# A convolution + GELU feed-forward kernel: block 0's x in half rows, W_in issued behind the mask, its copies split, and the first second-products moved ahead

## The chip, the cores and the metric

The kernel runs on one core of one Trainium2 chip. The metric is the device time in microseconds (us) of one execution of the program. "Span" is the time from the first to the last instruction in a profiled execution; the device time is about 1.7 us longer (682.34 against 680.6 in the first profile). All timed runs that are compared were fast, with a granted TensorE clock of 0.997 to 1.0. Each round of experiments ran on one chip together with its own runs of the kernel before, but the rounds used four different chips, so profiles of different rounds also differ in the chip. On one of these chips alone, 11 runs of the kernel before spread from 682.18 to 683.73 us.

## The reference

Eight sequences of 4096 tokens with 192 features pass a causal convolution of seven taps, one softmaxed set of weights per group of 24 features. The result goes through a feed-forward layer with an exact GELU.

```python
# x: (8, 4096, 192) f32, weight: (8, 7), w_in: (192, 2048), w_out: (2048, 192)
w = softmax(weight, axis=-1)
x_pad = concatenate([zeros((B, 6, D)), x], axis=1)
y[b, s, h, g] = sum_k w[h, k] * x_pad[b, s + k, h, g]      # the convolution
h = y.reshape(32768, 192) @ w_in                            # first product
out = gelu(h) @ w_out                                       # second product
```

## The kernel before

The tokens are two halves of 16384, and a block takes the same stretch of both: the first six blocks have 256 tokens of each half, the others 512. For each block, VectorE transposes x (32x32 blocks), the convolution makes `xc`, TensorE makes `hp` (first products), ScalarE the GELU `gT`, TensorE the second products in `ob`. Blocks 0 and 1 are convolved on TensorE (the "taps", `pconv`), block 2 onwards on VectorE: seven taps, 21 instructions a block.

The parts that the change and the argument touch, with cuts marked:

```python
def load(e, n, qs=(0, 2, 1, 3), sm=None):            # x of block n, four DMAs
    ...
        if n == 0:                                    # whole rows of 8 tokens, 96 columns of them not used
            dst = [[TB // 32 * DQ, 32], [1, mb * D - DQ]]
            src = [[mb * D, 32], [1, mb * D - DQ]]
        else:                                         # half rows of 384 bytes
            dst = [[TB // 32 * DQ, 32], [DQ, mb], [1, DQ]]
            src = [[D, 32], [32 * D, mb], [1, DQ]]

# GpSimd
win_in(FP[0], FP[1], S_WIN[0])                        # first pair of W_in's DMAs (f32 to bf16 on the way)
g.wait_ge(S_MSET, 1)
... affine_select x2 ...                              # the identity mask
for i in range(1, 3): win_in(FP[i], FP[i + 1], S_WIN[i])
halo(0); halo(1); ... casts of block 1 ...; casts of W_out

# VectorE
for p in range(NP): trans(0, p)
conv_out(v, 0, 1); conv_out(v, 0, 4)
dup(0); dup(1)                                        # copies of W_in to the other 64 partitions
for p in range(NP): trans(1, p)
dup(2)                                                # twice as wide
for j in range(len(PIECES)): conv_out(v, 1, j)        # evictions of block 1's taps
... then blocks 2, 3, ...: trans, 21 conv instructions ...

# SP (sync)
load(sp, 0, (0, 1)); sp.wait_ge(S_WIN[0], 32); load(sp, 1)
for i in range(4): ... W_out, a quarter each ...
load(sp, 2); load(sp, 3); ...

# TensorE
for i in range(NSL[n]):                               # 8 groups of a 256-token block
    mm1(n, i)                                         # 12 first-product matmuls
    for q in behind.get((n, i), []): pconv(*q)        # block 1's taps behind groups 4 and 5 of block 0
    for un in todo[a0:a1]: mm2(n - 1, *un)            # second products of the block before, by shares
```

`S_...` are semaphores. A first-product group writes one of two `hp` buffers, so group i waits for the GELU of group i - 2.

## Time and profile before

| | before |
|---|---|
| device time, median of 3 (then of 6) runs | 683.0 us (682.67 us) |
| span of the first profile | 680.6 us |
| chain that ended last | PE 98% |
| block 1's first group starts | 18.34 us |
| block 2's first group starts | 28.87 us |

The page shows what bounds the kernel as a whole: TensorE (PE). The prediction below quotes that page and the start of the chain. Two more views of the same profile matter for what follows, and the prediction did not use them.

The first is the table by stretches of the kernel before. Its columns are the stretch in us, its length, the busy time of PE, PEld, DVE, ACT and POOL (with counts), the granted clock, the mean busy share of the 16 DMA engines, and GB/s. Queues overlap, so the share can pass 1.

```profile
2.00:5.00 3.00, 3.00 (x8) 1.06 (x7) 2.05 (x10) 2.18 (x6) 2.85 (x7) 1.00 0.97 249
5.00:8.00 3.00, 2.71 (x42) 1.52 (x44) 1.58 (x4) 1.17 (x3) 2.19 (x7) 1.00 1.26 157
...
11.00:14.00 3.00, 2.53 (x38) 1.62 (x38) 1.23 (x3) 2.98 (x4) 0.64 (x2) 1.00 1.02 320
...
17.00:20.00 3.00, 2.59 (x50) 2.00 (x48) 2.11 (x7) 2.73 (x4) 1.31 (x3) 1.00 1.31 232
20.00:23.00 3.00, 3.00 (x70) 2.86 (x66) 2.96 (x9) 2.24 (x3) 0.32 (x1) 1.00 0.38 71
```

From 2 to 20 us the DMA engines are busy throughout (0.97 or more in every stretch, the two not shown here included); only then do they fall to 0.38.

The second is the timeline of the kernel before (start in us, length in us, engine, line, operation, count; in brackets the idle time of the engine just before and what ended it), where block 2 is made on VectorE and taken by TensorE:

```profile
19.24 1.35 DVE L529 STREAM_TRANSPOSE xT<-xin 128x256 f32<-128x256 f32 x3 [0.77 <-DMA xin<-in_x_dram]
27.35 1.27 DVE L562 SCALAR_TENSOR_TENSOR xc<-xT,wcol,acc 128x256 bf16<-128x256 f32 x3
28.87 0.82 PE L763 MATMUL hp<-xc,win 64*128 64x256 bf16 x12
```

VectorE waited for x of block 2 until 19.24, was busy without a gap for 9.38 us (until 27.35 + 1.27 = 28.62), and TensorE took the result at 28.87 without having waited. The two engines came to that point within 0.1 us of each other (VectorE by 28.78, as worked out under Theory A below); the chain view names only the one that came last.

### The profile page before, as it was taken

How to read it: one execution, taken by the hardware profiler on the slowest of the kernel's cores; microseconds unless marked ns; L12 is line 12 of the kernel's file. 1: busy time of each engine (PE TensorE's matmuls, PEld its weight loads, DVE VectorE, ACT ScalarE, POOL GpSimd, SP SyncE). 2: the span in 40 equal slices, each digit the busy share in tenths (PEclk: the TensorE clock that was granted, in tenths of full speed). 3: DMA queues.
4: the chain of work that ended last, by engine and by line, in shares of the span. 5: the costliest groups of instructions: out<-in, count | busy, mean ns of one | idle time of the engine just before them, and what ended most of it. 6: DMA issues, size and time to landing. Idle time of an engine off the chain costs nothing.

```text
span 680.6 us, 27316 instructions
## 1 busy us (share of the span) xinstructions
PE 674.6 (99%) x12576; PEld 407.5 (60%) x12576; DVE 561.7 (83%) x906; ACT 536.5 (79%) x548; POOL 38.9 (6%) x57
## 2 busy tenths in 40 slices
PE   8999999999999999999999999999999999999998
PEld 4999655555555555555555555555555555555557
DVE  6999989888889888899888898888898888988611
ACT  6899987787787877787777788777778777778772
POOL 5126000000000000000000000000000000000000
PEclk9999999999999999999999999999999999999999
DMA  9446233134442133331244422334322444310123
GB/s 223 88 99 138 64 71 81 43 69 95 96 94 61 45 87 94 95 89 46 59 95 94 94 70 45 78 94 96 89 56 47 95 94 96 80 40 25 48 50 94
DMA packets 132994, 54.79 MB, mean 81 GB/s; under 512 B 126480, under 2 KB 132752, under 8 KB 132880
## 3 DMA queue, kind: packets, MB, share of 16 engines
q1 hardware_dynamic: 130960, 51.50, 32.6%
q8 instruction: 98, 1.61, 1.0%
q0 software_dynamic: 1248, 0.79, 0.9%
q10 hardware_dynamic: 672, 0.76, 0.4%
q14 instruction: 16, 0.13, 0.1%
HBM read 28.66 MB, written 25.17 MB: 79 GB/s over the span
## 4 chain that ended last, share of the span: by engine, by line
PE 98%; ACT 1%; DMA 1%; DVE 0%; SPq 0%; issue 0%; ACTq 0%
PE hp L763 48%; PE ob L823 43%; PE ob L793 5%; PE hp L793 1%; DMA xin<-in_x_dram 1%; ACT gT L684 1%; PE ob L714 0%; ACT xc L191 0%; DVE xT L529 0%; ACT xTb L633 0%; SPq L871 0%; DVE osb L283 0%; SPq L332 0%; ACTq L632 0%
## 5 line engine op out<-in xcount | busy, mean ns | idle before, releaser
L684 ACT ACTIVATE gT<-hp 128x1024 bf16<-128x1024 f32 x512 | 523.2, 1024 | 129.0 <-PE hp L763 125.7
L763 PE MATMUL hp<-xc,win 64*64 64x512 bf16 (+2 forms) x6048 | 418.6, 366 | 1.5 <-ACT gT L684 1.1
L823 PE MATMUL ob<-gT,wout 64*64 64x512 bf16 x5376 | 366.3, 376 | 0.0
L562 DVE SCALAR_TENSOR_TENSOR acc<-xT,wcol,acc 128x512 f32<-128x512 f32 (+1 forms) x495 | 314.5, 699 | 0.0
L763 PEld LDWEIGHTS hp<-xc,win 64*64 64x64 bf16 (+1 forms) x6048 | 187.6, 106 | 136.1 <-ACT gT L684 2.6
L823 PEld LDWEIGHTS ob<-gT,wout 64*64 64x64 bf16 x5376 | 172.1, 118 | 123.0
L314 DVE STREAM_TRANSPOSE osb<-ob 128x512 f32<-128x512 f32 x84 | 74.1, 885 | 99.9 <-PE ob L823 99.9
L529 DVE STREAM_TRANSPOSE xT<-xin 128x512 f32<-128x512 f32 (+1 forms) x105 | 78.5, 797 | 3.4 <-DMA xin<-in_x_dram 3.4
L562 DVE SCALAR_TENSOR_TENSOR xc<-xT,wcol,acc 128x512 bf16<-128x512 f32 (+1 forms) x99 | 65.1, 712 | 0.0
L450 POOL COPY xT<-xT 128x18 f32<-128x18 f32 x30 | 27.9, 929 | 505.3 <-DVE xT L529 483.0
L793 PE MATMUL ob<-wout,gT 64*128 64x192 bf16 x896 | 46.8, 243 | 0.0
L793 PEld LDWEIGHTS ob<-wout,gT 64*128 64x128 bf16 x896 | 38.6, 94 | 5.2 <-issue 0.4
L555 DVE TENSOR_SCALAR acc<-xT,wcol 128x512 f32<-128x512 f32 (+1 forms) x90 | 37.5, 473 | 1.1
L698 PE MATMUL hp<-warm 128*128 128x512 bf16 x16 | 5.5, 516 | 1.3 <-DVE warm L466 1.3
L285 ACT ACTIVATE osb<-ob 128x192 f32<-128x192 f32 x2 | 0.7, 331 | 7.1 <-PE ob L793 7.1
L793 PE MATMUL hp<-wout,gT 64*128 64x192 bf16 x128 | 5.9, 243 | 0.0
L283 DVE COPY osb<-ob 128x192 f32<-128x192 f32 x2 | 0.7, 358 | 6.1 <-PE ob L793 6.1
L793 PEld LDWEIGHTS hp<-wout,gT 64*128 64x128 bf16 x128 | 5.3, 94 | 0.0
L657 ACT ACTIVATE acc<-xT,wcol 128x256 f32<-128x256 f32 (+1 forms) x9 | 5.2, 575 | 0.0
L270 ACT ACTIVATE osb<-ob 128x384 f32<-128x384 f32 x10 | 4.9, 486 | 0.0
L698 PEld LDWEIGHTS hp<-warm 128*128 128x128 bf16 x16 | 1.9, 126 | 4.3 <-issue 2.5
L387 POOL DMA_DIRECT2D win<-in_moe_w_in_dram x6 | 3.9, 660 | 0.8 <-POOLq L904 0.8
(36 smaller groups left out, 31.4 us busy)
## 6 DMA issues: line engine op xcount, KB each, us to landing
out_dram<-osb SPq DMA_DIRECT2D x122, 192.0 KB, 3.1
xin<-in_x_dram SPq DMA_DIRECT2D x116, 192.0 KB, 4.1
xin<-in_x_dram SPq DMA_DIRECT2D x20, 96.0 KB, 4.3
woutf<-in_moe_w_out_dram SPq DMA_DIRECT2D x4, 384.0 KB, 5.9
win<-in_moe_w_in_dram POOLq DMA_DIRECT2D x4, 96.0 KB, 4.6
win<-in_moe_w_in_dram POOLq DMA_DIRECT2D x2, 192.0 KB, 5.1
out_dram<-osb SPq DMA_DIRECT2D x8, 48.0 KB, 1.7
out_dram<-osb ACTq DMA_DIRECT2D x4, 96.0 KB, 2.0
```

Of the source, the lines that this page charges most:

```text
L270: e.activation(out=dst, in_=src, func=AF.Copy).then_inc(S_EVA)
L314: v.transpose(ap(osb[m % 2], j, [[8 * C, 128], [C // 2, TB // 32], [NP, 32]]), bank(ring(m, j)),).then_inc(S_EV)
L450: g.tensor_copy(dst, src).then_inc(S_HALO)
L529: v.transpose(ap(xT[n % 2], p * XW + HX, [[NP * XW, 128], [1, w]]), ap(xin[n % NX], p, [[TB // 32 * DQ, 128], [D if n == 0 else DQ, w // 3 ...
L555: ins = v.tensor_scalar(a, src, wk, None, ALU.mult)
L562: ins = v.scalar_tensor_tensor(dst, src, wk, a, op0=ALU.mult, op1=ALU.add)
L657: a.activation(out=acc[n % 2][:, p * TB : p * TB + w], in_=ap(xT[n % 2], p * XW + HX, [[NP * XW, 128], [1, w]]), func=AF.Copy, scale=wcol[ ...
L684: a.activation(out=ap(gT[n % 2], i * c * 2 * w, dst), in_=ap(hp[u % 2], 0, src), func=AF.Gelu,).then_inc(S_GELU)
L698: t.matmul(hp[1][:, 0:512], warm[:, 0:128], warm[:, :])
L763: ins = t.matmul(hp[u % 2][fo : fo + fw, o : o + w], ap(win, f1, [[NP * F, 64], [2, fw]]), xc[n % 2][r, p * TB : p * TB + w], start=(p == ...
L793: ins = t.matmul(bb[sub], gT[m % 2][r, c0 : c0 + 128], wout[r, CH[sub][i] * C : (CH[sub][i] + 1) * C], start=(ph == 0 and i == 0), stop=(p ...
L823: ins = t.matmul(bank(ring(m, j), slice(64 * h, 64 * h + 64), w), ap(wout, 64 * hf * NF * C + CH[h][i] * C + j, [[NF * C, 64], [NP, 64]],) ...
```

## The change

The intent is to shorten the start. Block 0's x is fetched without the columns that nobody uses; GpSimd makes the mask first and issues W_in afterwards; the last, double-width copy of W_in is split in two, with one piece in VectorE's wait ahead of block 1; four of the 16 warm-up matmuls go; and four "units" of second products (8 matmuls) run ahead of block 1's first group, with the chunks of W_out's first half first. The diff, cut to its core:

```diff
-                    dst = [[TB // 32 * DQ, 32], [1, mb * D - DQ]]
-                    src = [[mb * D, 32], [1, mb * D - DQ]]
+                dst = [[TB // 32 * DQ, 32], [DQ, mb], [1, DQ]]
+                    src = [[mb * D, 32], [D, mb], [1, DQ]]
...
-            win_in(FP[0], FP[1], S_WIN[0])
             g.wait_ge(S_MSET, 1)
...
-            for i in range(1, 3):
-                win_in(FP[i], FP[i + 1], S_WIN[i])
...          (in halo(0), behind its memset)
+                    for i in range(3):
+                        win_in(FP[i], FP[i + 1], S_WIN[i])
...
-            dup(0)
-            dup(1)
+            for i in range(3):
+                dup(i)
             for p in range(NP):
                 trans(1, p)
-            dup(2)
+            dup(3)
...
-            for i in range(16):
+            for i in range(12):
...
-            share = {1: [4, 12, 8, 8, 8, 8, 8, 8]}
+            share = {1: [4, 12, 9, 9, 10, 5, 5, 6]}
+            AHEAD = 4
...
+                if m == 0:
+                    us.sort(key=lambda q: not (q[1] == 0 and q[2] < 4))
...
+                if n == 0:
+                    results(0, units(0)[:AHEAD])
```

More of the change, by code (lines that the diff above doesn't have):

```diff
@@ L324, in load @@
                 off = ((q // 2) * HALF + OFF[n]) * D + DQ * (q % 2)
+                dst = [[TB // 32 * DQ, 32], [DQ, mb], [1, DQ]]
                 if n == 0:
-                    dst = [[TB // 32 * DQ, 32], [1, mb * D - DQ]]
-                    src = [[mb * D, 32], [1, mb * D - DQ]]
+                    src = [[mb * D, 32], [D, mb], [1, DQ]]
                 else:
-                    dst = [[TB // 32 * DQ, 32], [DQ, mb], [1, DQ]]
                     src = [[D, 32], [32 * D, mb], [1, DQ]]
@@ L501, in dup @@
             def dup(s):
-                v.wait_ge(S_WIN[s], 32)
+                v.wait_ge(S_WIN[min(s, 2)], 32)
                 for hf in range(2):
@@ L507, in dup @@
                             win,
-                            64 * (1 - hf) * NP * F + FH + FP[s],
-                            [[NP * F, 64], [F, NP], [1, FP[s + 1] - FP[s]]],
-                        ),
-                        ap(
-                            win,
-                            64 * hf * NP * F + FP[s],
-                            [[NP * F, 64], [F, NP], [1, FP[s + 1] - FP[s]]],
-                        ),
+                            64 * (1 - hf) * NP * F + FH + FQ * s,
+                            [[NP * F, 64], [F, NP], [1, FQ]],
+                        ),
+                        ap(win, 64 * hf * NP * F + FQ * s, [[NP * F, 64], [F, NP], [1, FQ]]),
                     ).then_inc(S_DUPE)
@@ L533, in trans @@
                         p,
-                        [[TB // 32 * DQ, 128], [D if n == 0 else DQ, w // 32], [NP, 32]],
+                        [[TB // 32 * DQ, 128], [DQ, w // 32], [NP, 32]],
                     ),
@@ L748, in mm1 @@
                     t.wait_ge(S_WIN[i], 32)
-                if n == 0 and 4 <= i < 7:
+                if n == 0 and i >= 4:
                     t.wait_ge(S_DUPE, 2 * (i - 4) + 2)
@@ L843, in units, with results @@
                     return [(ps, i) for ps in range(3) for i in range(NF)]
-                return [
-                    (g, ph, i) for g in range(NG[m]) for ph in range(2) for i in range(NF)
-                ]
+                us = [(g, ph, i) for g in range(NG[m]) for ph in range(2) for i in range(NF)]
+                if m == 0:
+                    us.sort(key=lambda q: not (q[1] == 0 and q[2] < 4))
+                return us
+            def results(m, us):
+                for un in us:
+                    if m == 0 and un in ((0, 0, 0), (0, 0, 4)):
+                        t.wait_ge(S_WOG, 2 + un[2] // 2)
+                        t.wait_ge(S_PCE, 2 + 3)
+                    (mm2_t if M0 <= m < M1 else mm2)(m, *un)
             for n in range(NB):
                 todo = units(n - 1) if n >= 1 else []
+                ws = SHARE if M0 < n <= M1 else share.get(n, [1] * NSL[n])
+                if n == 1:
+                    todo = todo[AHEAD:]
                 for i in range(NSL[n]):
@@ L853, in _ @@
                         pconv(*q)
-                    new = M0 < n <= M1
-                    ws = SHARE if new else share.get(n, [1] * NSL[n])
                     a0 = len(todo) * sum(ws[:i]) // sum(ws)
                     a1 = len(todo) * sum(ws[: i + 1]) // sum(ws)
-                    for un in todo[a0:a1]:
-                        if n == 1 and un in ((0, 0, 0), (0, 0, 4)):
-                            t.wait_ge(S_WOG, 2 + un[2] // 2)
-                        (mm2_t if new else mm2)(n - 1, *un)
+                    results(n - 1, todo[a0:a1])
+                if n == 0:
+                    results(0, units(0)[:AHEAD])
             m = NB - 1
```

## The prediction

> **What bounds the kernel now.** First the page of the profile, for which engine carries the span. Its chain of work that ended last says:
>
> ```profile
> PE 98%; ACT 1%; DMA 1%; DVE 0%; SPq 0%; issue 0%; ACTq 0%
> PEclk9999999999999999999999999999999999999999
> ```
>
> TensorE is the chain for 98% of 680.6 us at the full granted clock. So I went on to the same chain in order of time, cut to the first 60 us, to find where TensorE still waits (columns: start in us, length in us, what):
>
> ```profile
> 1.64 4.26 DMA xin<-in_x_dram
> 5.93 0.54 DVE xT L529
> 6.55 0.42 ACT xTb L633
> 7.02 0.97 PE ob L714 x18
> 9.45 0.63 PE hp L763 x8
> 10.10 1.94 ACT gT L684 x2
> 14.22 0.95 PE ob L714 x26
> 17.26 1.03 ACT gT L684
> 18.34 0.83 PE hp L763 x12
> 19.17 0.33 PE ob L793 x8
> 19.50 0.65 PE hp L763 x12
> ```
>
> The reader is to see three stretches. Up to 7.02 us the first x block is fetched (4.26 us of DMA), transposed and cast. From 7.02 to 18.34 TensorE takes turns with ScalarE: a group of 12 first matmuls takes 0.65 us, the GELU over it 1.03 us, and there are two buffers between them, so TensorE waits. From 18.34 on, 12 first-product and about 16 second-product matmuls per GELU (0.66 + 0.66 us against 1.03) leave no wait; every later piece of that view up to 60 us is PE. Therefore the whole change is worth: how much earlier the point "18.34" comes, plus the TensorE work that is moved ahead of it. Nothing after 20 us has a wait to lose.
>
> Why the 18.34 is where it is, from the timeline of the first 20 us:
>
> ```profile
> 2.81 0.56 POOL L396 TENSOR_SCALAR_AFFINE_SELECT idb<-idb 64x64 bf16<-64x64 bf16 x2
> 3.30 2.53 POOL L387 DMA_DIRECT2D win<-in_moe_w_in_dram  x4
> 4.62 0.63 DVE L494 TENSOR_TENSOR dg<-idb,wcol 128x448 bf16<-128x448 bf16 x1
> 6.52 1.16 POOL L417 CAST xTb<-xT 128x186 bf16<-128x186 f32 x3 [0.47 <-DVE xT L529]
> 12.77 1.34 DVE L529 STREAM_TRANSPOSE xT<-xin 128x256 f32<-128x256 f32 x3 [1.93 <-DMA xin<-in_x_dram]
> 14.15 2.00 DVE L505 COPY win<-win 64x1536 bf16<-64x1536 bf16 x2
> 15.98 1.02 ACT L684 ACTIVATE gT<-hp 128x1024 bf16<-128x1024 f32 x1 [0.95 <-PE hp L763]
> 16.17 2.29 DVE L193 CAST xc<-ob 128x256 bf16<-128x256 f32 x6
> 17.26 3.96 ACT L684 ACTIVATE gT<-hp 128x1024 bf16<-128x1024 f32 x4 [0.25 <-PE hp L763]
> ```
>
> Eight GELUs of block 0 start at 10.10. ScalarE loses 0.95 us before the sixth, because block 1's tap matmuls (L714, 14.22) stand ahead of that matmul group in TensorE's order and wait for block 1's x (VectorE idle 1.93 us until it lands, 12.77), and 0.25 us before the seventh, where the last quarter pair of W_in copies (2.00 us, until 16.15) and the tap matmuls end together.
>
> **What the Trainium skill says.** "TensorE: Matmul & The Clock Gate", Part 1, gives a warm-up of about 3.4 us of time, not a number of matmuls. The trace agrees roughly: the 128x512 warm matmuls start at 1.26 us, about 0.43 us apart until 5.05 and faster after it, so the switch came after some 3.8 us, at the ninth or tenth of 16. Twelve are enough. "DMA: Bandwidth & Descriptors", Latency, gives a first byte after about 0.6 us for a DMA issued by sync or scalar and 1 us by GpSimd. Here the trace is slower: x is issued at 0.88 and its first packet starts at 1.90 (1.0 us); W_in's fifth DMA is issued at 4.59 and starts at 6.67 (2.1 us), its first took 3.0 us beside x. The same page's Specifications want 512 B or more per transfer for line rate; here 384 B rows of later blocks pass at some 600 packets per us (231 GB/s) and block 0's 5760 B packets at 128 in 3.18 us with W_in beside them at the end (232 GB/s), so in this case the short rows cost little.
>
> **The change part by part.**
> 1. Half rows for block 0. Before: four DMAs of 180 KB (128 packets of 5760 B), almost half of it not used; packets from 1.90 to 5.08, landed 5.90. After: four of 96 KB, 1024 packets of 384 B. At 600 per us that is 1.7 us; the last DMA is issued at 1.64, so it can't begin before about 2.9. I put the last packet near 3.9, and the landing 0.8 us later (5.08 to 5.90 before), 4.7. But VectorE has the mask product dg ahead of the transposes, which ends at 5.25 and hangs on the softmax, not on the mask (wcol, until 4.58). So the first transpose moves from 5.93 to 5.27: 0.66 us, not 1.2.
> 2. W_in behind the mask. GpSimd: mask from about 1.3 to 1.85, halo memset to about 2.2, six issues at 0.78 + 5 x 0.63 = 3.9, so until 6.1 (before: 5.83). The halo copies of block 0 follow in order: first at 6.1 instead of 6.52. This caps the gain at about 0.45 us: the first tap needs the cast (5.84 + 0.42 = 6.26), the second tap the halo (6.1 + 0.35 = 6.45). So the taps start at about 6.5 instead of 7.02, and the first GELU at 9.6 instead of 10.10. The first half W_in pair starts about 2.1 us after its issue at 2.2, at 4.3 as before, but without x beside it; 0.55 us each and spacing by issue gives 5.6 for its last packet instead of 5.83.
> 3. Block 1's x is issued when that pair has landed: 6.4 instead of 6.68. Its packets ran from 8.96 to 12.18 among W_in's last packets (until 10.33); with W_in through at about 9.3 to 9.8 I expect x of block 1 at 12.0 to 12.4 instead of 12.77. GpSimd's casts and the taps of block 1 move with it: 0.4 to 0.7 us.
> 4. Copies of W_in. Third quarter (0.9 us) now into VectorE's 1.93 us wait, fourth (0.9 us instead of 2.00) behind the transposes. The work is the same; the VectorE block ahead of block 1's evictions (16.17) shrinks by 1.0 us, so they start when their taps are done, about 15. That takes away the limit on groups 7 and 8; the gap of 0.25 us should shrink to nothing or follow the taps.
> 5. Twelve instead of 16 warm matmuls: they end at about 5.75 (9 x 0.43 + 3 x 0.22 after 1.26) instead of 6.72. Taken alone nothing, but 16 would hold the taps until 6.72, so it lets through the last 0.2 us of item 2.
> 6. Four second-product units (8 matmuls) go between the last first-product group of block 0 and block 1's first. There TensorE waits now: group 8 ends at 17.93 and the next waits for the GELU until 18.34. By the row above 8 such matmuls take 0.33 us, and 0.41 us are free. Their W_out quarters are cast from 14.78 on, two at 0.83 to 1.02 us, done by 16.7, and block 1's banks 0 and 1 are evicted by about 16: no new wait. Gain 0.33 us. Four units of the other half next (sort) only push back the need for the second half of W_out. The new shares keep 1.06 us of TensorE per GELU at the end of block 1 against 1.03 us of ScalarE, with one eviction of 0.49 us among them: I went through the two buffers by hand and found no wait over 0.1 us.
>
> Sum: 0.45 (taps earlier, passed on through the GELU chain) + 0.33 (units ahead) + 0.2 (part of the 1.2 us of GELU gaps that goes with items 3 and 4; all of it is not to be had, for the taps of block 1, 0.95 + 0.52 us, still stand in TensorE's order) = about 1.0 us. 683.0 - 1.0 = 682.0.
>
> **Rivals.**
> - GpSimd becomes the limit of the start. It issues six DMAs in a row before block 0's halo; each 0.1 us more per issue is 0.6 us later. Against: four issues back to back took 2.53 us in the trace. If it did, the taps start no earlier than 7.0 and only the 0.33 us and item 4 are left: 682.5.
> - W_in becomes the limit. Its first issue moves from 1.32 to about 2.2; if its latency of 3.0 us was its own and not x's doing, the first pair lands 0.6 us later, block 1's x with it, and the saving at the start is given back at block 1's taps: 682.6 to 683.0. For it: the first DMA did start 3.0 us after issue. Against: x filled the engines until 5.08, and later ones needed 2.1.
> - The DMA relief is larger. 353 KB less before W_in, and nothing of x beside it: x of block 1 lands by 11.8, its taps are ready when group 5 ends, the gap of 0.95 us falls to 0.4 (the tap matmuls themselves): 1.5 us in all, 681.5.
> - The whole is hidden anyway: not likely, as the chain shows no slack, but the share of 683 us is small in any case.
>
> **Range and chances.** The known waits ahead of 18.34 that the change touches are 0.66 at the start, 1.2 in the GELU gaps and 0.41 behind group 8; all of them together would be some 2.2 us, 0.3%. 2% is 13.7 us, which no part can give, and nothing here can cost that much short of a stall in every block. The runs before scatter by 0.6 us, and I add that to the rivals' 681.5 to 682.8: 681.2 to 682.9.
>
> **What would show it.** Right: first transpose of x at 5.3 and right behind dg; halo casts on GpSimd right behind its last issue near 6.1; taps at 6.5; first GELU at 9.6; block 1's transposes near 12.2; 8 second-product matmuls ahead of block 1's first group; no TensorE wait from about 17.8. Wrong: VectorE waiting for x after 5.3 (short packets slower than thought), GELU gaps of 1 us or more left or new ones at groups 2 or 3 (W_in late), a wait for W_out's casts, or ScalarE-bound gaps at the end of block 1.

## The result, and the profile after

| | before | after |
|---|---|---|
| device time, median | 682.67 us (682.09 to 683.24, 6 runs) | 683.14 us (682.47 to 683.35, 6 runs) |
| ratio of the fast runs | | 1.0005, 95% interval 0.9992 to 1.0017 |
| span of the first profile | 680.6 us | 681.6 us |
| first transpose of block 0 / 1 / 2 | 5.93 / 12.77 / 19.24 | 6.35 / 12.76 / 20.37 |
| block 1's first group starts | 18.34 | 18.42 |
| block 2's first group starts | 28.87 | 29.91 |

A ratio is the mean time of one kernel's fast runs over that of the other's of the same rounds, so it is not quite the ratio of the medians quoted.

The time is the same within noise. 683.14 us lies above the range of 681.2 to 682.9, so the microsecond that was expected did not come. The page of the changed kernel gives the first hint, in its chain of work that ended last:

```profile
PE 95%; DMA 2%; DVE 1%; SPq 1%; issue 0%; POOL 0%
```

VectorE and the DMAs, which held 1% between them before, now hold 3%. The chain leaves TensorE at one place. The timeline of the changed kernel shows where:

```profile
6.35 1.34 DVE L522 STREAM_TRANSPOSE xT<-xin 128x256 f32<-128x256 f32 x3 [1.09 <-DMA xin<-in_x_dram]
6.93 1.17 POOL L414 CAST xTb<-xT 128x186 bf16<-128x186 f32 x3 [1.03 <-DVE xT L522]
...
12.76 1.35 DVE L522 STREAM_TRANSPOSE xT<-xin 128x256 f32<-128x256 f32 x3 [0.61 <-DMA xin<-in_x_dram]
15.29 2.29 DVE L193 CAST xc<-ob 128x256 bf16<-128x256 f32 x6 [0.28 <-PE ob L707]
16.06 1.02 ACT L677 ACTIVATE gT<-hp 128x1024 bf16<-128x1024 f32 x1 [0.63 <-PE hp L756]
18.00 0.51 PE L786 MATMUL ob<-wout,gT 64*128 64x192 bf16 x8
20.37 1.35 DVE L522 STREAM_TRANSPOSE xT<-xin 128x256 f32<-128x256 f32 x3 [2.78 <-DMA xin<-in_x_dram]
28.49 1.27 DVE L555 SCALAR_TENSOR_TENSOR xc<-xT,wcol,acc 128x256 bf16<-128x256 f32 x3
29.91 0.83 PE L756 MATMUL hp<-xc,win 64*128 64x256 bf16 x12 [1.12 <-DVE xc L555]
```

The reader is to see four things. Block 0's x came later (VectorE idle 1.09 us, until 6.35), not earlier. Block 1's evictions do start earlier (15.29 against 16.17), as intended, and the gap ahead of the sixth GELU shrank from 0.95 to 0.63 us. The eight matmuls ahead are there at 18.00. And then TensorE waits 1.12 us for VectorE's convolution of block 2, because VectorE had waited 2.78 us for its x.

The sum closes: the taps started 0.41 us later (7.43 against 7.02), the GELU gaps gave 0.31 us back, so block 1's first group came 0.1 us later; the units ahead were worth 0.33 us, so TensorE was free for block 2 some 0.25 us earlier; and the wait turned this into a start 1.04 us later (29.91 - 28.87). The spans differ by 1.0 us. The same table by stretches of the changed kernel shows the DMA engines:

```profile
2.00:5.00 3.00, 3.00 (x8) 1.06 (x7) 2.04 (x10) 2.17 (x6) 3.00 (x6) 1.00 0.79 155
5.00:8.00 3.00, 1.95 (x19) 0.88 (x21) 1.60 (x4) 1.04 (x3) 1.83 (x5) 1.00 1.16 139
...
17.00:20.00 3.00, 2.98 (x58) 2.28 (x56) 0.56 (x2) 2.73 (x4) 1.09 (x3) 1.00 1.28 223
20.00:23.00 3.00, 3.00 (x70) 2.86 (x66) 2.59 (x8) 2.33 (x3) 0.32 (x1) 1.00 0.60 119
```

They are less full from 2 to 5 us (0.79 against 0.97) and busier past 20 us (0.60 against 0.38): the transfers as a whole end later, although 0.35 MB less is read (28.31 against 28.66 MB on the two pages).

### The profile page after: what moved, and what is told of

It is laid out like the page before. It is cut to its first block, busy times and chain, and to the rows that moved or that the text cites. A ratio compares the mean times of both kernels' runs of the same rounds, so it can differ in the third digit from the quotient of the medians.

```text
span 681.6 us, 27311 instructions
## 1 busy us (share of the span) xinstructions
PE 674.2 (99%) x12572; PEld 410.2 (60%) x12572; DVE 560.9 (82%) x908; ACT 536.5 (79%) x548; POOL 38.6 (6%) x57
## 3 DMA queue, kind: packets, MB, share of 16 engines
HBM read 28.31 MB, written 25.17 MB: 78 GB/s over the span
## 4 chain that ended last, share of the span: by engine, by line
PE 95%; DMA 2%; DVE 1%; SPq 1%; issue 0%; POOL 0%
PE hp L756 47%; PE ob L818 43%; PE ob L786 5%; DMA xin<-in_x_dram 1%; DVE acc L555 1%; PE hp L786 1%; SPq L330 1%; DMA win<-in_moe_w_in_dram 1%; SPq L882 0%; DVE xT L522 0%; DVE acc L548 0%; DVE xc L555 0%; POOL win L385 0%; POOL idb L393 0%; DVE osb L283 0%
## 5 line engine op out<-in xcount | busy, mean ns | idle before, releaser
L677 ACT ACTIVATE gT<-hp 128x1024 bf16<-128x1024 f32 x512 | 523.1, 1024 | 129.7 <-PE hp L756 126.4
L756 PEld LDWEIGHTS hp<-xc,win 64*64 64x64 bf16 (+1 forms) x6048 | 189.9, 106 | 135.2 <-ACT gT L677 3.1
L786 PEld LDWEIGHTS ob<-wout,gT 64*128 64x128 bf16 x896 | 40.0, 94 | 3.9 <-issue 0.4
L707 PE MATMUL ob<-xTb,dg 64*64 64x256 bf16 (+1 forms) x112 | 3.2, 245 | 1.1 <-ACT xTb L626 1.1
L193 DVE CAST xc<-ob 64x256 bf16<-64x256 f32 (+3 forms) x8 | 2.8, 357 | 1.5 <-PE ob L707 1.4
```

The lines of the kernel that those rows point to most:

```text
L677: a.activation(out=ap(gT[n % 2], i * c * 2 * w, dst), in_=ap(hp[u % 2], 0, src), func=AF.Gelu,).then_inc(S_GELU)
L756: ins = t.matmul(hp[u % 2][fo : fo + fw, o : o + w], ap(win, f1, [[NP * F, 64], [2, fw]]), xc[n % 2][r, p * TB : p * TB + w], start=(p == ...
L786: ins = t.matmul(bb[sub], gT[m % 2][r, c0 : c0 + 128], wout[r, CH[sub][i] * C : (CH[sub][i] + 1) * C], start=(ph == 0 and i == 0), stop=(p ...
```

## The experiments

**Theory A** (formed on the two traces): the span is 651.7 us plus the start of block 2's first group. That start is the later of two chains: TensorE's own, and the landing of x of block 2 plus VectorE's 9.54 us (20.37 to 29.91). Before, they met within 0.1 us (19.24 + 9.54 = 28.78 for VectorE against 28.87); the change moved x of block 2 later. **Rival B**: W_in's later issue makes everything behind it late. **Rival C**: the new order of TensorE's units makes the wait.

Sixteen runs were made: thirteen edited kernels and three repeats of the two unaltered ones. The profiles gave these numbers (us). "W_in" is the last packet of W_in's third part by the trace's packet records. "Held by" is how long TensorE waited for it, as the profile records waits; since matmul ends are modelled, a wait of up to some 0.3 us can be missing (how this shows is said in the point-by-point part). "Free" marks the two edits in which block 2 doesn't wait for its own x.

| kernel | x of block 0 | W_in order | block 0 transposed | W_in | held by W_in | block 1 transposed | block 2 transposed | held by VectorE | block 2's first group | span |
|---|---|---|---|---|---|---|---|---|---|---|
| before | full | old | 5.93 | 10.33 | 0 | 12.77 | 19.24 | 0 | 28.87 | 680.6 |
| before, again | full | old | 5.93 | 10.81 | 0.62 | 13.11 | 20.06 | 0.19 | 29.58 | 681.3 |
| after | half | new | 6.35 | 10.88 | 0 | 12.76 | 20.37 | 1.12 | 29.91 | 681.6 |
| after, again | half | new | 5.96 | 11.06 | 0.83 | 12.99 | 20.03 | 0.62 | 29.55 | 681.3 |
| after, third | half | new | 5.93 | 10.89 | 0.69 | 13.64 | 20.12 | 0 | 29.65 | 681.4 |
| e1 | full | new | 5.91 | 10.21 | 0 | 12.53 | 19.11 | 0 | 28.63 | 680.3 |
| e2 | half | old | 6.70 | 9.70 | 0 | 11.99 | 19.06 | 0 | 29.31 | 681.0 |
| e3 | half | old | 6.71 | 9.89 | 0 | 12.55 | 19.97 | 0.34 | 29.50 | 681.2 |
| e4 | half | new | 5.96 | 12.00 | 1.73 | 14.45 | 20.55 | 0 | 35.36 | 687.0 |
| e5 | half | new | 5.85 | 11.17 | 1.02 | 13.41 | 20.12 | 0 | 29.99 | 681.7 |
| e6 | half | new | 5.96 | 11.36 | 1.12 | 13.62 | (free) 18.32 | 0 | 29.40 | 681.1 |
| e7 | full | old | 6.03 | 10.25 | 0 | 12.51 | (free) 18.25 | 0 | 28.64 | 680.3 |
| e8 | full | new | 5.84 | 10.11 | 0 | 12.50 | (free) 17.18 | 0 | 28.27 | 680.0 |
| e9 | full | new | 5.96 | 9.87 | 0 | 11.96 | 19.04 | 0 | 29.17 | 680.9 |
| e10 | full | old | 5.88 | 10.65 | 0.57 | 12.92 | 20.21 | 0.86 | 29.74 | 681.5 |
| f1 | half | behind x | 5.17 | 14.63 | 0 | 17.15 | 24.58 | 1.02 | 34.12 | 685.8 |
| f2 | full | new | 6.10 | 10.07 | 0 | 12.85 | 18.23 | 0 | 30.37 | 682.1 |
| f3 | full | old | 6.04 | 10.43 | 0 | 13.35 | 19.09 | 0 | 30.47 | 682.2 |

In every row the span less the start of block 2's first group is 651.7, to 0.05 us. So whatever the change did, it did before block 2, and the start of block 2's first group can be read in place of the time.

### e1: full rows again

```diff
-                    src = [[mb * D, 32], [D, mb], [1, DQ]]
+                    dst = [[TB // 32 * DQ, 32], [1, mb * D - DQ]]
+                    src = [[mb * D, 32], [1, mb * D - DQ]]
...          (and the transposes' reading pattern to match)
```

> The changed kernel with block 0's x in full rows again (part 1 undone, all else kept). Theory A (x of block 2 lands late, VectorE's convolution of block 2 then holds TensorE: span = 651.7 us + the later of TensorE's arrival and block 2's first transpose + 9.54): if the short rows are what delays the DMA engines, block 0's first transpose comes at 5.3 to 5.9 instead of 6.35 and block 2's at about 19.2 to 19.6 instead of 20.37, TensorE's wait at block 2 shrinks from 1.1 us to 0.3 or less, and the time falls by 0.7 to 1.0 us against the changed kernel. Rival B (W_in's later issue delays the DMA chain): block 2's transpose stays near 20.4 and the wait stays at 1.1 us. Rival C (the order of TensorE's units makes the wait): the same 1.1 us wait whatever x does.

Measured: 683.18 us (682.07 to 683.57) against 682.87 before, ratio 1.0002 (0.9990 to 1.0014). In its profile no wait for VectorE is recorded and the span is 680.3. Its timeline:

```profile
5.91 1.32 DVE L523 STREAM_TRANSPOSE xT<-xin 128x256 f32<-128x256 f32 x3 [0.66 <-DMA xin<-in_x_dram]
19.11 1.34 DVE L523 STREAM_TRANSPOSE xT<-xin 128x256 f32<-128x256 f32 x3 [1.90 <-DMA xin<-in_x_dram]
28.63 0.83 PE L757 MATMUL hp<-xc,win 64*128 64x256 bf16 x12
```

The profile went as theory A said; TensorE was free at about 28.3 and took block 2 when VectorE was ready, 19.11 + 9.52 = 28.63. The gain expected in the median did not show: the profiled execution is the fastest of five (682.07), and the others were up to 1.5 us longer. That was the first sign that landings vary from run to run by as much as the effect. Rival B alone does not hold in this profile: W_in was issued as late as in the changed kernel, and x of block 2 was still there at 19.11.

### e2: the kernel before with half rows alone

```diff
-                    dst = [[TB // 32 * DQ, 32], [1, mb * D - DQ]]
-                    src = [[mb * D, 32], [1, mb * D - DQ]]
+                    src = [[mb * D, 32], [D, mb], [1, DQ]]
...          (and the transposes' reading pattern to match)
```

> The kernel before with block 0's x in half rows and nothing else. Theory A with short rows to blame: block 0's transpose no earlier than 5.9, block 2's later than 19.24 (to about 20.2), a TensorE wait for VectorE at block 2 of up to 1 us, time up to 1 us longer than before. Rival B (W_in's later issue to blame): block 0's transpose at 5.3 to 5.9, block 2's at 19.2 or earlier, no wait, time the same as before or 0.3 us less.

Measured: 683.23 us against 682.87, ratio 1.0006 (0.9994 to 1.0018). Neither expectation was right. Block 0 was transposed 0.77 us later than before (6.70), while W_in, block 1 and block 2 came earlier (9.70, 11.99, 19.06). TensorE itself was late at block 2 (29.31). The short rows hand time from block 0's x to W_in: in the packet records W_in's first packet starts at 2.82 instead of 4.29, among x's packets.

### e3: W_in's first pair ahead of the mask again

```diff
+            win_in(FP[0], FP[1], S_WIN[0])
             g.wait_ge(S_MSET, 1)
...
-                    for i in range(3):
+                    for i in range(1, 3):
```

> The changed kernel with W_in's first pair issued ahead of the mask again (part 2 undone, short rows kept). Theory A with W_in's place to blame: W_in's and block 1's x land 0.5 us or more earlier (block 1's transpose at 12.0 to 12.3, as in the run with short rows alone: 11.99), block 2's first transpose at 19.0 to 19.3, no TensorE wait at block 2, but block 0's first transpose later, at 6.5 to 6.8, since W_in then runs among x's packets. Time within 0.4 us of the changed kernel. With short rows alone to blame: block 2's transpose stays at 20 or later.

Measured: 683.05 us against 682.91, ratio 1.0004 (0.9990 to 1.0017). Block 0 was as expected (6.71) and W_in came earlier (9.89), but block 1 (12.55) and block 2 (19.97) were transposed later than expected, and TensorE waited 0.34 us at block 2. With e2 it shows that in half rows the old order costs block 0 some 0.7 us, and the new order costs W_in 1 us or more (9.70 and 9.89 against 10.88 and later). It also shows a limit of these profiles: in e2 and e3 both DMA parts are set alike, and yet x of block 2 was transposed at 19.06 in the one and 19.97 in the other.

### e4: x of block 2 between the halves of W_out

```diff
             for i in range(4):
                 g = WG[i]
+                if i == 2:
+                    load(sp, 2)
...
-            load(sp, 2)
```

> The changed kernel with x of block 2 issued between the two halves of W_out instead of behind them. Theory A: block 2's first transpose moves from 20.37 to about 17.6 to 18.2 (behind block 1's evictions), TensorE's wait for VectorE at block 2 is gone; the second half of W_out lands 1 us or more later and TensorE may wait 0.3 to 1 us for its casts near 20 us; net 0.1 to 0.9 us faster than the changed kernel. Rival C (TensorE's order, not x, is at fault): TensorE still waits about 1 us at block 2 or before it and the time is the same.

A miss: 684.7 us against 682.87, ratio 1.0037 (1.0017 to 1.0057), and runs up to 688.77. The list of TensorE's waits in its profile (who, what for: us in total, times, longest):

```profile
PE ob L786 <- POOL wout L457: 2.5, 1, 2.5
PE hp L756 <- DMA win<-in_moe_w_in_dram: 1.7, 1, 1.7
```

W_out's last two casts came at 22.31 and 24.25, and x of block 2 not even earlier (20.55). Putting one transfer forward pushed another back by more. The profile is that of the slowest of the six runs: W_in was later in it (12.00) than in any other but f1, and the granted clock was 0.50 from 26 to 29 us, behind the wait of 2.5 us.

### e5: without the units ahead

```diff
-            share = {1: [4, 12, 9, 9, 10, 5, 5, 6]}
+            share = {1: [4, 12, 8, 8, 8, 8, 8, 8]}
-            AHEAD = 4
+            AHEAD = 0
-                    us.sort(key=lambda q: not (q[1] == 0 and q[2] < 4))
+                    pass
```

> The changed kernel without the four units ahead, the sort and the new shares (the order of the kernel before). Theory A: VectorE sets block 2's start, so the 0.33 us of work done ahead only lengthens the wait; without it the wait at block 2 shrinks from 1.1 to about 0.8 us and the time stays within 0.2 us. Rival C (the new order makes the wait): the wait is gone and the time falls by 0.7 us or more. If the units ahead count in full: the time rises by 0.33 us.

Measured: 683.6 us against 682.87, ratio 1.0014 (1.0001 to 1.0027); the changed kernel stood at 1.0005 in other rounds. Rival C falls: without the new order the time did not drop. But theory A's "within 0.2 us" is not borne out either. In this profile TensorE, not VectorE, set block 2 (29.99 against 20.12 + 9.54 = 29.66). W_in was late (TensorE waited 1.02 us for it), but that is not enough to explain it. In the last group of block 0 TensorE also stood idle for 0.61 us without a wait that the profile shows ("issue"):

```profile
19.04 0.95 PE L756 MATMUL hp<-xc,win 64*128 64x256 bf16 x14 [0.61 <-issue]
```

These are the last two matmuls of that group, which had started at 17.71, and block 1's first 12. In the kernel before block 1's first group starts 1.28 us after the last group of block 0, and block 2's 10.53 us after that; without the idle time TensorE would so have come to block 2 at about 29.5 (an estimate), before VectorE. What the idle time comes from is open, and so this run doesn't show what the units ahead are worth.

### e6, e7: block 2 freed of its x (wrong results on purpose)

Block 2 is transposed from block 1's x, which has long landed; the DMA of its own x still runs. The same edit on the changed kernel (e6) and on the kernel before (e7):

```diff
-                    if xin_at(n) > 0:
+                    if n != 2:
                         v.wait_ge(S_XIN[n % NX], xin_at(n))
+                    if n == 3:
+                        v.wait_ge(S_XIN[2], 64)
...
-                        xin[n % NX],
+                        xin[1 if n == 2 else n % NX],
...          (in load)
-                e.wait_ge(S_TR, NP * (n - NX + 1))
+                e.wait_ge(S_TR, NP * (n - NX + 1) + {4: NP, 5: 1}.get(n, 0))
```

> The changed kernel, wrong on purpose: block 2 is transposed from block 1's x, which has long landed, so nothing waits for x of block 2 (its DMA still runs; two later loads wait a little longer so that no buffer is overwritten). Theory A: block 2's first transpose starts right behind block 1's evictions, at 17.5 to 18.5 instead of 20.37, VectorE's convolution ends about 27.5, TensorE's wait of 1.1 us at block 2 is gone and block 2's first products start at 28.6 to 28.8 instead of 29.91; the span is 0.9 to 1.3 us shorter than the changed kernel's profile of 681.6, and 0.2 to 0.3 us shorter than the same edit on the kernel before. The runs scatter less. Rival (TensorE's own order or the shares hold it): a wait of about 1 us stays.

> The kernel before with the same edit, wrong on purpose in the same way. Theory A: in the profile of the kernel before TensorE did not wait, it came to block 2 within 0.1 us of VectorE, so in a run like that the gain is 0 to 0.2 us (span 680.4 to 680.6); but if in other runs of it x of block 2 lands later, the median falls by 0.2 to 0.5 us and the scatter shrinks. Rival: no change of the time at all.

Measured: e6 682.85 us against 682.91 (ratio 1.0000, 0.9988 to 1.0013); e7 682.47 against 682.91 (ratio 0.9994, 0.9981 to 1.0006), with all five runs within 0.5 us. Neither profile has a wait for VectorE. The kernel before gains 0.44 us in the median, as theory A said for runs in which block 2's x is late, though the interval still holds 1. The changed kernel missed its expectation: block 2's first group started at 29.40 instead of 28.6 to 28.8, and the span was 0.8 us longer than in e7 instead of 0.2 to 0.3 us shorter. The reason was not in the theory; it is in the timeline of e6:

```profile
11.86 1.49 PE L758 MATMUL hp<-xc,win 64*128 64x256 bf16 x24 [1.12 <-DMA win<-in_moe_w_in_dram]
```

TensorE waits 1.12 us at the third group of block 0 for the third part of W_in. Block 1's first group starts at 19.20 for it, against 18.11 in e7. From there to block 2 it takes 10.20 us in e6 and 10.53 in e7: the 0.33 us of the units ahead, as predicted.

### r1, r2, r3: both kernels again, unaltered

> The changed kernel once more, unaltered, for a second profile. If the landing of x of block 2 varies from run to run, block 2's first transpose is at another time than 20.37 and the span follows it: span = 651.7 us + the later of (that transpose + 9.54) and about 28.6.

> The kernel before once more, unaltered, for a second profile: if x of block 2 lands at another time than in the first (first transpose 19.24), the span is 651.7 us + the later of (that transpose + 9.54) and about 28.8.

> The changed kernel, unaltered, third profile: W_in's third part late (last packet 10.9 or later, TensorE waits up to 1 us for it at group 3) or block 2's first transpose at 20 or later with a TensorE wait for VectorE, or both; span 681 to 681.7.

All three came as expected; they took no edit. The second profile of the kernel *before* is the telling one. Its timeline:

```profile
11.34 1.59 PE L763 MATMUL hp<-xc,win 64*128 64x256 bf16 x24 [0.62 <-DMA win<-in_moe_w_in_dram]
18.69 0.83 PE L763 MATMUL hp<-xc,win 64*128 64x256 bf16 x12 [0.45 <-ACT gT L684]
20.06 1.34 DVE L529 STREAM_TRANSPOSE xT<-xin 128x256 f32<-128x256 f32 x3 [1.25 <-DMA xin<-in_x_dram]
29.58 0.83 PE L763 MATMUL hp<-xc,win 64*128 64x256 bf16 x12 [0.19 <-DVE xc L562]
```

The same kernel waits for W_in and for VectorE, and its span is 681.3. The profile that the prediction was made from was a good draw: 0.7 us below this one, and with 682.34 us some 0.3 us below the median of the six runs (682.67). The three profiles of the changed kernel are at 681.3 to 681.6.

### e8: full rows, and block 2 freed of its x (wrong on purpose)

e1's edit and e6's together.

> The changed kernel with full rows for block 0 and, wrong on purpose, block 2 transposed from block 1's x: both suspected costs taken away at once. Theory A' (short rows make W_in and block 2's x late; VectorE then holds block 2): no wait for W_in at group 3, no wait for VectorE, block 2's first products at 28.2 to 28.4 (28.32 is where TensorE was free in the run with full rows), span 679.9 to 680.1, time 681.6 to 682.1, that is 0.3 to 0.5 us less than the same edit on the kernel before (682.47): the units ahead, 0.33 us, then count. Rival (the rest of the change is worth nothing): the same as the kernel before with that edit, span 680.3, 682.5 us.

Measured: 682.27 us against 682.97, ratio 0.9991 (0.9977 to 1.0004); span 680.0, no wait for W_in and none for VectorE, and block 2's first group as expected:

```profile
28.27 0.82 PE L759 MATMUL hp<-xc,win 64*128 64x256 bf16 x12
```

In e7 it started at 28.64. The median is above the 681.6 to 682.1 that were expected. Against their own rounds of before, e7 gained 0.44 us and e8 0.70: the right sign for the 0.33 us of units ahead, though the interval still holds 1. With both costs away, what is left of the change is worth about 0.3 us in the span (680.3 to 680.0).

### e9: a version meant to beat both

Full rows, x of block 2 ahead of W_out's last quarter, and TensorE's first units from all chunks of W_out's first half.

```diff
+                if i == 3:
+                    load(sp, 2)
...
-                    us.sort(key=lambda q: not (q[1] == 0 and q[2] < 4))
+                    us.sort(key=lambda q: not (q[1] == 0 and q[2] // 4 % 2 == 0))
-            share = {1: [4, 12, 9, 9, 10, 5, 5, 6]}
+            share = {1: [4, 8, 13, 9, 10, 5, 5, 6]}
```

> A right kernel meant to beat both: the changed kernel with full rows, x of block 2 issued ahead of the last quarter of W_out, and TensorE's first units taken from both W_out chunks groups that the first half holds (units 0 to 3 and 8 to 11 of both halves), so that the last quarter is needed about 1.3 us later. Theory A': block 2's first transpose at 17.6 to 18.5, the last W_out cast ends by 20.8, no TensorE wait, block 2's first products at 28.2 to 28.4, time 681.7 to 682.3. If the DMA engines are slowed by the new order (as in the run with x between the halves): W_out's last cast after 21.5, a TensorE wait of 0.5 us or more, 683 or more.

Measured: 682.62 us against 682.97, ratio 0.9996 (0.9983 to 1.0008): not told apart from before. W_out's last cast started at 20.66 and TensorE waited 0.37 us for it; x of block 2 was transposed at 19.04, hardly earlier than in e1 and not at the 17.6 to 18.5 expected. Block 2's first group started at 29.17, later than in e1 (28.63). The results are right, but no gain is shown.

### e10: without both DMA parts

e1's and e3's edits together: full rows, W_in's first pair ahead of the mask.

> The changed kernel with both DMA parts undone (full rows, W_in's first pair ahead of the mask); what is left is the copies of W_in, 12 warm matmuls, the units ahead and the shares. Theory A': DMA as in the kernel before, block 0's first transpose 5.9, block 2's 19.1 to 19.4; TensorE comes to block 2 about 0.35 us earlier (28.3 to 28.5) and waits there for VectorE 0.2 to 0.5 us, so the start of block 2 stays at 28.7 to 28.9 and the time within 0.2 us of the kernel before. Rival (the units ahead count in full): 0.33 us or more faster than before.

Measured: 683.19 us against 682.97, ratio 1.0003 (0.9991 to 1.0016). Here the DMAs are those of the kernel before, and they landed as late as in its second profile (W_in 10.65, block 2's x 20.21; 19.1 to 19.4 was expected). From its timeline:

```profile
29.74 0.83 PE L758 MATMUL hp<-xc,win 64*128 64x256 bf16 x12 [0.86 <-DVE xc L557]
```

TensorE was ready 0.86 us early and waited for VectorE. In the kernel before with nearly the same landings (second profile) it waited 0.19. The work done ahead lengthened the wait, as expected; the rival, that it counts in full, falls in this profile. The interval of the times is too wide to decide it: 0.33 us is 0.0005.

### f1: block 0's x alone

```diff
+                    g.wait_ge(S_XIN[0], 64)
                     for i in range(3):
                         win_in(FP[i], FP[i + 1], S_WIN[i])
```

> The changed kernel with all of W_in held back until block 0's x has landed (only to measure x alone; the kernel gets slower, since W_in comes later). If W_in's packets among it were what delayed x: its last packet at about 4.2 (it was at 5.4 to 5.8), landed by 5.0, first transpose at 5.3 right behind the mask product. If the short rows' own issue and transfer cost that much: last packet still after 5.2 and first transpose at 5.8 or later.

Measured, in one look (687.59 us, slower, as it had to be). Its timeline:

```profile
5.17 1.32 DVE L523 STREAM_TRANSPOSE xT<-xin 128x256 f32<-128x256 f32 x3
5.23 3.89 POOL L385 DMA_DIRECT2D win<-in_moe_w_in_dram  x6 [3.11 <-DMA xin<-in_x_dram]
```

The first transpose stands behind the mask product without any wait, 0.1 us earlier than the 5.27 that was predicted for the change. x's last packet ended at 4.60 (5.46 to 5.83 in the changed kernel's three profiles, with W_in's packets from 3.65 to 3.8 on). So it is W_in's packets among x's that hold x back. The short rows' own time was more than predicted too (4.60 instead of 3.9), but VectorE's mask product hides that.

### f2, f3: x of block 2 from GpSimd's queue

Right results. On the changed kernel with full rows (f2) and on the kernel before (f3), block 2's x is issued from GpSimd behind `halo(1)`, where GpSimd is idle:

```diff
             halo(1)
+            load(g, 2, sm=S_X2)
...
-            load(sp, 2)
...
-                    if xin_at(n) > 0:
+                    if n == 2:
+                        v.wait_ge(S_X2, 64)
+                    else:
                         v.wait_ge(S_XIN[n % NX], xin_at(n))
...          (and the counts of S_XIN[2] to match)
```

> A right kernel: the changed one with full rows for block 0, and block 2's x issued by GpSimd, which is idle from 7.8 to 13 us, into its own queue beside W_out instead of by SP behind it. Theory A': x of block 2 lands by 16, its first transpose follows block 1's evictions at 17.2 to 18, TensorE never waits for VectorE at block 2, first products of block 2 at 28.3, span 680.0, time 681.7 to 682.3 as in the wrong-on-purpose run with full rows (682.27). If the new queue slows block 1's x or W_out: block 1's transpose later than 13 or W_out's last cast after 20, and 682.7 or more.

> The kernel before with block 2's x issued by GpSimd in the same way. Theory A': like the wrong-on-purpose run of the kernel before (682.47, span 680.3): 682.3 to 682.7, 0.3 us more than f2_full_x2_gpsimd, which does four units ahead. Rival (x of block 2 was no limit): no change against the kernel before.

Both slower: f2 683.85 us against 682.89 (ratio 1.0017, 1.0004 to 1.0029), f3 684.18 (ratio 1.0020, 1.0006 to 1.0033). f2's timeline:

```profile
18.23 1.35 DVE L527 STREAM_TRANSPOSE xT<-xin 128x256 f32<-128x256 f32 x3 [0.73 <-DMA xin<-in_x_dram]
20.93 0.83 POOL L460 CAST wout<-woutf 128x768 bf16<-128x768 f32 x1 [0.98 <-DMA woutf<-in_moe_w_out_dram]
21.81 1.16 PE L791 MATMUL ob<-wout,gT 64*128 64x192 bf16 x24 [1.54 <-POOL wout L460]
```

x of block 2 came earlier (18.23) and TensorE no longer waited for VectorE. But W_out came later by more, its last cast at 20.93 (17.75 in e1), and TensorE waited 1.54 us for that; in f3 the last cast was at 20.56 and the wait 0.7 us. The second expectation, that the new queue slows W_out, is what happened. The Trainium skill says it on its page "DMA: Bandwidth & Descriptors", section "Issuing engines are not separate DMA queues": DMAs started by different engines run on the same 16 DMA engines and interleave. This trace agrees, with the 1.54 us as its price.

## Why the prediction was wrong, point by point

- **"Nothing after 20 us has a wait to lose", and with it "the whole change is worth: how much earlier the point "18.34" comes, plus the TensorE work that is moved ahead of it".** This is the step that failed first. VectorE's chain ended within 0.1 us of TensorE's at block 2 (28.78 against 28.87), so at most 0.1 us could pass unless x of block 2 also landed earlier, and it didn't: 20.03 to 20.37 in the changed kernel's three profiles, 19.24 and 20.06 before. A chain view shows only the branch that came last. TensorE's recorded waits there were 1.12, 0.62 and 0 us, and 0.86 in e10, where no DMA part was changed.
- **How far VectorE held block 2.** From block 1's first group to block 2's TensorE alone needs 10.53 us in the old order of units (e7) and 10.20 in the new (e6, e8). Added to the start of block 1's first group (18.42, 18.56 and 19.20 in the changed kernel's three profiles) this gives, as an estimate, 28.62, 28.76 and 29.40 for TensorE alone. The group started at 29.91, 29.55 and 29.65, each time 9.52 to 9.54 us after VectorE's first transpose of that block. So VectorE set the start in all three, by 1.29, 0.79 and 0.25 us; the recorded waits are some 0.2 us too short, and the 0 of the third profile is such a case.
- **The rival "The whole is hidden anyway", dismissed because "the chain shows no slack".** This rival is the nearest to what came. The slack that was missing in the chain was VectorE's, which the view doesn't show.
- **Part 1, "the last packet near 3.9", landing 4.7.** It ended at 5.46 to 5.83, and the first transpose came at 5.93 to 6.35 instead of 5.27. Two terms are mis-sized. The short rows alone take until 4.60 (f1), not 3.9: 1024 packets in 2.23 us are about 460 per us, not 600. And W_in, which I took to start at 4.3 "without x beside it", starts at 3.65 to 3.8 among x's packets, which accounts for the other 0.9 to 1.2 us. The second is the one that counts, for in f1 the first transpose came at 5.17. So the gain of 0.45 us at the start was 0 in two profiles and a loss of 0.4 in the first.
- **Part 2 and the rivals on GpSimd and on W_in.** GpSimd was no limit: its six issues ended at 5.90. W_in's first pair landed in time. The third part did not: its last packet came at 10.88 to 12.00 in the six profiles with half rows and the new order, and TensorE waited 0.69 to 1.73 us at the third group in five of them. The prediction gave the rival "W_in becomes the limit" the wrong victim (block 1's x, at most 683.0), and named new gaps "at groups 2 or 3 (W_in late)" only as a sign of error. Each part alone made W_in no later than before (full rows and new order 9.87 to 10.21; half rows and old order 9.70 and 9.89; before's combination 10.25 to 10.81). Why both together are the worst is open: the records don't say which DMA engine a packet was on.
- **Part 3, block 1's x at 12.0 to 12.4.** It came at 12.76 to 13.64 in the changed kernel's three profiles, before at 12.77 and 13.11. In e8 and e9 (full rows) it came at 12.50 and 11.96.
- **Part 4, the copies.** Half right. The evictions started at 15.29 instead of 16.17 (15.35 and 15.99 in the other two profiles), and in the first profile the gap ahead of the sixth GELU was 0.63 instead of 0.95 us. But the gap of 0.25 us ahead of the seventh, which was to shrink to nothing, stayed at 0.26 in all three, and where x of block 1 was late (13.64) the gap ahead of the sixth was 1.60.
- **Part 5, twelve warm matmuls.** In the first profile they ran at 0.43 us each to the end, until 6.37 us instead of the 5.75 predicted (5.93 and 6.56 in the other two). The Trainium skill's page "TensorE: Matmul & The Clock Gate", Part 1, calls the count run-variable; I had used one trace's. It cost nothing here, as the taps came at 7.43 and took the same 1.69 us.
- **Part 6, the units ahead.** Right in size: 0.33 us between e6 and e7. Right in place, too. Where VectorE holds block 2 they only lengthen the wait (e10).
- **The range.** It was built from one profile of the kernel before and the scatter of its times. The landings of the same kernel differ by 0.8 us between two profiles (19.24 and 20.06), and the first was a lucky one. Medians of "before" in later rounds were 682.87 to 682.97; a change whose effect is below 0.5 us can't be placed without several profiles. The upper end also took 682.8 for the rivals, where the rival on W_in had been put at up to 683.0. Two smaller slips change nothing: the bytes saved are 344 KB (737,280 - 393,216 bytes), not 353, and the sum for the warm matmuls gives 5.79, not 5.75.

What is shown: the time follows the start of block 2's first group; in the changed kernel's three profiles VectorE's work on block 2 sets that start, so what TensorE gained ahead of it could not pass; and W_in is later with half rows and the new order together (10.88 or more in six profiles, 10.81 or less in the other eleven, f1 left out). With block 2 freed and full rows the units ahead are seen in the profile (28.27 in e8 against 28.64 in e7), but the intervals of the timed runs still hold 1.

What is not shown: that the change makes x of block 2 later. It does so against the first profile of the kernel before (19.24), not against the second or e10 (20.06 and 20.21). Nor is it shown that a right kernel could keep the gain. In e2, e4, f2 and f3 an earlier transfer was paid for with a later one, and e9 won nothing that the interval shows. A relief of VectorE's 9.5 us on block 2, in place of an earlier x, was not tried.

## What to carry to other kernels

Where a chain view shows one engine without waits, look for the second chain that ends just before it: work out for each consumer when its other inputs were ready, for a gain passes only until the next of them is met. Where the DMA engines are busy over a whole stage, as here from 2 to 20 us, ask of each transfer moved forward which other one it moves back (here W_out in e4, f2 and f3, and x of block 0 in e2). Fewer bytes were no sure gain either: check what the freed slots are filled with. And take the spread of landings from several profiles of the kernel before, ahead of a prediction in tenths of a microsecond.

## What the Trainium skill lacked or had wrong

- "DMA: Bandwidth & Descriptors", Latency, has one first-byte figure for a DMA from sync or scalar (about 0.6 us). Here it was 1.0 us with 32 rows of 5760 B (issued 0.88, first packet 1.90) and 1.5 us with 256 rows of 384 B (0.88 to 2.36). The issuing instruction itself grew with the rows, from 0.39 and 0.44 us to 0.70 and 0.62 us on ScalarE's queue; I found no figure for that on the page.
- The same page gives no spread of landings. Two profiles of one kernel had the last packet of W_in's third part at 10.33 and 10.81 and block 2's x ready at 19.24 and 20.06 us.
- The same page's Specifications ask for 512 B or more per transfer for line rate. That agrees in direction; I found no measured rate for rows of 384 B on it. Alone, 1024 packets of 384 B took from 2.37 to 4.60 us (f1), which is 176 GB/s, where block 0's rows of 5760 B took from 1.90 to 5.08 us (before), 232 GB/s with W_in beside them at the end. In a later block the same 384 B rows passed at about 230 GB/s, so the row length alone doesn't set the rate.
- No page that I read warns that a chain of waits followed back from the end hides a second chain 0.1 us behind it; here that was the first step that failed (28.78 against 28.87).
